# Turning the maxima of the half chunk with 128-row products, and inverting the column sums once

## The chip, the cores and the metric

The kernel runs on one core of a Trainium2 chip. A core has engines that run side by side and meet only at semaphores: TensorE (PE in the profile) multiplies matrices and writes to PSUM; VectorE (DVE) and ScalarE (ACT) compute elementwise and reduce, and carry results from PSUM to SBUF; GpSimd (POOL) computes on SBUF and issues most DMAs here; SyncE (SP) issues the rest. Each engine takes its instructions in the order in which the program lists them. The metric is the time of one execution on the device in microseconds (us).

## The reference

Attention with an extra term in the denominator, for 8 batches of 12 heads, 448 tokens and 64 dimensions, and then a mixture of experts with soft slots (8 experts of 4 slots, 768 wide, hidden layer of 1024), over the 3584 tokens of all batches.

```python
scores = scale * np.matmul(q, k.transpose(0, 1, 3, 2))
m = np.max(scores, axis=-1, keepdims=True)
e = np.exp(scores - m)
attn = e / (np.sum(e, axis=-1, keepdims=True) + np.exp(-m) + 1e-09)
x = np.matmul(attn, v)                       # then (batch, token) x (head, dim)

logits = x @ phi                             # 3584 x 32
d = np.exp(logits - logits.max(0, keepdims=True))
d /= d.sum(0, keepdims=True) + 1e-09
slot_input = (d.T @ x).reshape(E, S_per_e, D)
slot_out[e] = np.maximum(slot_input[e] @ w1[e], 0.0) @ w2[e]
c = np.exp(logits - logits.max(1, keepdims=True))
c /= c.sum(1, keepdims=True) + 1e-09
out = c @ slot_out
```

The maximum `m` of each row of scores and the sum of `c` over the 32 slots are what the change touches.

## The kernel before

**Tiles.** Heads are taken in pairs: 48 pairs `n`, six for each batch, and three pairs make a group `g` (`NP = 3`). The two heads of a pair (`hl` 0 and 1) lie in the two halves of the 128 partitions. The 448 rows of a head are cut into three chunks of 128 and one of 64; the 64-row "half chunks" of the two heads share one tile, head 0 in partitions 64 to 127 and head 1 in 0 to 63.

**Steps for a pair.** `T` turns q and k (TensorE L251, evicted by VectorE L257 or ScalarE L255). `A` and `A1` compute scores by row into `ps_a` (L274, L283, L291), from which VectorE takes the row maxima (`reduce_max`, L277, L285, L292) into one column of `wm`. `wm` has 4 x 128 columns for a group: chunk `i` in columns 128 `i` onward, head `hl` at 64 `hl`, pair `n % 3` behind that. Two `wm` tiles alternate; both are zeroed once at the start. `Bk` and `AB` compute the scores once more, turned, into `ps_b` (L337, L359), subtract the maxima by a product with `sel` (L340, L362), and ScalarE takes the exponential (L343, L364). `AV` multiplies by v (L397), `N1` evicts (L409), `N2` takes the reciprocal of the row sums on VectorE (L418, L419) and scales on POOL (L423, L427, L428), and `PX` turns the result (L449, evicted at L455).

**Turning the maxima.** Once for each group (17 times) `W2` turns `wm` into rows: three products with `ident` (L299) for the 128-row chunks, each a weight tile of 128 rows and 128 columns, and two products of 64 rows and 64 columns (L302) for the half chunk, one for each head. `W3` copies the result to `mT` (ScalarE L307) and computes the extra term of the denominator (`ec`, L311, L314).

**Work per batch.** `P(b)` holds the router's steps: logits (L475), their maxima, exponentials, sums for the slots (L543), and `c_turn`: TensorE turns the exponentials `cd` (L548), VectorE copies them to `cT` (L549), sums them over the slots into `crec[:, b, :]` (L551), adds 1e-9 (L552) and takes the reciprocal (L553). `crec` is 128 x 8 batches x 4 in fp32. It is read only after the hidden layer of the experts, by the products of L840 which move it to `cscale`.

**Order.** The whole order is written out by hand. A loop over `s` (48 pairs) with two half-steps `y` emits, in this order, `AB` and `Bk` for pair `s`, `A1` for a later pair between their products, `T(s + 6)`, and at `y = 1`, for every third `s`, `W2` and `W3` of the next group; then `AV` of pair `s`, then the step of `P` that `post` lists for this half-step, then `PX(s - 2)` and `N2`. `c_turn` of batches 0 to 5 falls in the half-step of `s = 6b + 11`, which has a `W2` as well. After the loop come the last batch's steps, the experts (`hidden`, `turn`, `slots`, `pick`) and the output. PSUM has 3 buffers for `ps_a` and `ps_t` (psA), 4 for `ps_b`, `ps_m` and `ps_x` (psB), and one for `ps_av`.

Of the kernel before, what the change touches and what calls it, by code (L numbers as in the profile page):

```python
# [10 lines left out]
AX = mybir.AxisListType  # L11
AF = mybir.ActivationFunctionType
ALU = mybir.AluOpType
# [12 lines left out]
NP = 3  # L26
W65 = 65
VS = 66


@with_exitstack
def kernel(
# [10 lines left out]
    nc = tc.nc  # L43
    B, H, S, D = q.shape
# [11 lines left out]
    scale = 1.0 / (D ** 0.5)  # L56
# [9 lines left out]
    crec = keep.tile([128, B, 4], F32, name="crec")  # L66
    acc = keep.tile([128, KC + 1, NS], F32, name="acc")

    ident = const.tile([128, 128], BF16, name="ident")
# [8 lines left out]

    NQK, NE, VPN, NATV = 7, 5, HG * 4 * VS, HG * 4 * D
    sizes = [("nq0", 2 * NP * S), ("nq1", 2 * NP * S), ("nv", NATV), ("qk6", 2 * S), ("wm1", 512),  # L80
# [13 lines left out]
    wm = [part(f"wm{i}", 0, 512).rearrange("p (i c) -> p i c", i=4) for i in range(2)]  # L94
# [48 lines left out]
    with ExitStack() as at:  # L143
# [118 lines left out]
        mg = lambda n: 0 if n == 0 else n // NP + 1  # L262

        def top(n, i, hl=0):
            c = 64 * hl + n % NP
            return wm[mg(n) % 2][:, i, c:c + 1]

        def A(n, i):
            t = qkT[n]
            if i < 3:  # L270
                pss = [psA.tile([128, 512], F32, tag="a", name="ps_a") for _ in range(2)]
                for hl in range(2):
                    r = slice(64 * hl, 64 * hl + 64)
                    nc.tensor.matmul(pss[hl][:, 0:S], t[r, 0, i * 128:(i + 1) * 128], t[r, 1, :],  # L274
                                     start=True, stop=True)
                for hl in range(2):
                    nc.vector.reduce_max(top(n, i, hl), pss[hl][:, 0:S], axis=AX.X)  # L277
            else:
                ps = psA.tile([128, 512], F32, tag="a", name="ps_a")

                for hl in range(2):
                    r = slice(64 * hl, 64 * hl + 64)
                    nc.tensor.matmul(ps[64 - 64 * hl:128 - 64 * hl, 0:S], t[r, 0, 384:448], t[r, 1, :],  # L283
                                     start=True, stop=True)
                nc.vector.reduce_max(top(n, i), ps[:, 0:S], axis=AX.X)  # L285

        def A1(n, i, hl):

            t, r = qkT[n], slice(64 * hl, 64 * hl + 64)
            ps = psA.tile([128, 512], F32, tag="a", name="ps_a")  # L290
            nc.tensor.matmul(ps[:, 0:S], t[r, 0, i * 128:(i + 1) * 128], t[r, 1, :], start=True, stop=True)  # L291
            nc.vector.reduce_max(top(n, i, hl), ps[:, 0:S], axis=AX.X)  # L292


        def W2(g):
            w = wm[g % 2]
            ps = pb_("ps_m")
            for i in range(3):
                nc.tensor.matmul(ps[:, i * 128:(i + 1) * 128], w[:, i, :], ident, start=True, stop=True)  # L299
            for hl in range(2):  # L300
                r = slice(64 - 64 * hl, 128 - 64 * hl)
                nc.tensor.matmul(ps[64 * hl:64 * hl + 64, 384:448], w[r, 3, 0:64], ident[r, r], start=True, stop=True)  # L302
            st["ps_m"] = ps

        def W3(g):
            t = psm.tile([128, S], BF16, tag="mT", name="mT")
            nc.scalar.copy(t, st["ps_m"][:, 0:S])  # L307
            mT[g] = t
            e = psm.tile([128, NP, 7], F32, tag="ec", name="ec", bufs=3)
            w = wm[g % 2]  # L310
            nc.scalar.activation(e[:, :, 0:6].rearrange("p l (i h) -> p i l h", i=3),  # L311
                                 w[:, 0:3, :].rearrange("p i (h c) -> p i c h", h=2)[:, :, 0:NP, :],
                                 AF.Exp, scale=-scale)
            nc.scalar.activation(e[:, :, 6], w[:, 3, 0:NP], AF.Exp, scale=-scale)  # L314
            ec[g] = e


# [144 lines left out]
        def P(b):  # L462
# [3 lines left out]
            v = {}  # L466
# [79 lines left out]
            def c_turn():  # L546
                ps = pa([128, 128], BF16, "ps_ct")
                nc.tensor.transpose(ps, flat(v["cd"][:, 0:4, :]), ident)  # L548
                nc.vector.tensor_copy(cT[:, b // 2, :, b % 2, :], ps.rearrange("p (h j) -> p h j", h=2))  # L549
                r = crec[:, b, :]  # L550
                nc.vector.reduce_sum(r, v["cd"][:, 0:4, :], axis=AX.X)  # L551
                nc.vector.tensor_scalar(r, r, 1e-9, None, op0=ALU.add)  # L552
                nc.vector.reciprocal(r, r)  # L553

            def s_add():
                if b:
# [68 lines left out]
        warm(1, S)  # L625
        As(2)
        W2(0)
        W3(0)
        V(0)
        load(1, "v")  # L630
# [15 lines left out]
        for s in range(NPAIR):  # L646
            for y in range(2):
# [18 lines left out]
                if y == 0:  # L666
                    if 0 <= s - 1:
                        for i in (2, 3):
                            AV(s - 1, i, range(3))
                else:  # L670
                    if 2 <= s < NPAIR - 6:
                        T(s + 6)
                    g = (s + 1) // 3
                    if (s + 1) % 3 == 0 and g < NG:
                        W2(g + 1)
                        W3(g + 1)
                    if s < NPAIR:
                        for i in (0, 1):
                            AV(s, i, range(3))
# [19 lines left out]
                if hs == 1:  # L699
                    W2(1)  # L700
                    W3(1)
# [26 lines left out]
        n = NPAIR - 1  # L728
# [107 lines left out]
        for half in range(2):  # L836
            ps = psA.tile([128, 512], F32, tag="a", name="ps_cs")
            r = slice(64 * half, 64 * half + 64)
            for b2 in range(2):
                nc.tensor.matmul(ps[64 * b2:64 * b2 + 64, 0:2 * B], identf[r, r], crec[r, b2::2, :],  # L840
                                 start=True, stop=True)
# [54 lines left out]
```

## Time and profile before

| | us |
|---|---|
| median of three runs | 308.73 |
| their range | 307.33 to 309.12 |
| the profiled execution | 309.52 |
| its span, first to last instruction | 307.7 |

| stage (us of the span) | length | TensorE busy | VectorE busy | ScalarE busy | POOL busy |
|---|---|---|---|---|---|
| first pairs (0 to 40) | 40 | 37.0 | 34.3 | 27.0 | 27.4 |
| 40 to 240 | 200 | 196.3 | 188.2 | 189.0 | 147.5 |
| 240 to 260 | 20 | 19.3 | 13.4 | 17.3 | 10.0 |
| experts (260 to 280) | 20 | 17.4 | 9.0 | 7.9 | 0.0 |
| output (280 to 308) | 28 | 9.3 | 12.2 | 9.9 | 0.0 |

The stages are sums of the profile's windows. From 40 to 240 us, where the pairs follow one another, three engines are busy for 94% of the time or more, and TensorE's granted clock is full. "Busy" for TensorE counts a product until it has left the array, so that products in flight together count once, and a wait shorter than that tail does not show as idle. VectorE and ScalarE overlap the tail of one instruction with the head of the next by 0.08 to 0.15 us when the second does not depend on the first.

### The profile page before, as it was taken

The numbers are of one execution on the slowest core, as the hardware profiler recorded it, in microseconds if no ns is written. First come the engines' busy times: TensorE is split into PE (matmuls) and PEld (weight loads), VectorE is DVE, ScalarE is ACT, GpSimd is POOL, SyncE is SP. The second block draws the span as 40 slices with busy tenths as digits, with TensorE's granted clock in tenths as the row PEclk, the third lists the DMA queues.
The fourth block names the chain that finished last, engine by engine and source line by source line (L and its number), as shares of the span: only waits on it lengthen the run. The fifth ranks groups of instructions, "written<-read, shape, count | busy, mean of one in ns | idle before, by whom it ended". The sixth has DMA issues, their size and how long they took to land.

```text
span 307.7 us, 12173 instructions
## 1 busy us (share of the span) xinstructions
PE 279.3 (91%) x5097; PEld 159.8 (52%) x5097; DVE 257.1 (84%) x604; ACT 250.9 (82%) x551; POOL 184.9 (60%) x336
## 2 busy tenths in 40 slices
PE   7999999999999999999999999999999999995900
PEld 2444656566565656555656565656564555441100
DVE  7899999999999999989999999999999676446910
ACT  3477999999999999989999999999999995345800
POOL 9681986968586869866877677686747662000000
PEclk9999999999999999999999999999999999997555
DMA  8999999999999999999999999999845899909995
GB/s 134 134 158 184 139 210 202 195 197 165 191 161 198 164 200 148 202 184 151 120 202 134 197 179 204 151 200 205 141 56 88 124 137 224 362 32 341 433 426 229
DMA packets 49384, 57.69 MB, mean 188 GB/s; under 512 B 2865, under 2 KB 41521, under 8 KB 48945
## 3 DMA queue, kind: packets, MB, share of 16 engines
q0 software_dynamic: 45280, 42.29, 89.6%
q1 hardware_dynamic: 4048, 14.62, 12.1%
q8 instruction: 40, 0.66, 0.8%
q14 instruction: 16, 0.12, 0.1%
HBM read 88.18 MB, written 14.16 MB: 333 GB/s over the span
## 4 chain that ended last, share of the span: by engine, by line
PE 69%; DVE 14%; ACT 8%; issue 3%; POOL 1%; DVEq 0%; POOLq 0%
PE ps_av L397 15%; PE ps_a L291 9%; PE ps_t L251 7%; PE ps_b L359 7%; PE ps_b L362 6%; DVE R L292 6%; PE ps_b L337 4%; PE ps_b L340 2%; ACT R L343 2%; DVE R L277 2%; PE ps_x L449 2%; PE ps_o L802 2%; PE ps_a L274 2%; PE ps_so L773 2%; ACT R L255 2%
## 5 line engine op out<-in xcount | busy, mean ns | idle before, releaser
L292 DVE TENSOR_REDUCE R<-ps_a 128x1 bf16<-128x448 f32 x254 | 140.0, 615 | 6.4 <-PE ps_a L291 5.5
L364 ACT ACTIVATE R<-ps_b 128x448 bf16<-128x448 f32 x272 | 131.0, 573 | 0.5 <-PE ps_b L362 0.2
L291 PE MATMUL ps_a<-R 64*128 64x448 bf16 x254 | 83.2, 353 | 1.5 <-DVE R L292 1.5
L359 PE MATMUL ps_b<-R 64*128 64x448 bf16 x272 | 74.5, 353 | 1.1
L362 PE MATMUL ps_b<-mT,sel 64*128 64x448 bf16 x272 | 71.3, 350 | 0.0
L423 POOL TENSOR_TENSOR R<-ubuf,rec 128x384 bf16<-128x384 f32 x44 | 36.2, 823 | 55.1 <-DVE rec L419 33.7
L397 PEld LDWEIGHTS <-R 128*128 128x128 bf16 (+1 forms) x1536 | 50.0, 100 | 30.8 <-issue 26.1
L397 PE MATMUL ps_av<-R 128*128 128x65 bf16 (+1 forms) x1536 | 64.6, 196 | 0.0
L343 ACT ACTIVATE R<-ps_b 128x448 bf16<-128x448 f32 x64 | 35.9, 579 | 2.7 <-PE ps_b L340 2.6
L251 PEld LDWEIGHTS <-R 64*64 64x64 bf16 x1344 | 30.0, 112 | 12.6 <-issue 4.9
L455 ACT CAST R<-ps_x 128x512 bf16<-128x512 f32 x47 | 28.1, 599 | 6.9 <-PE ps_x L449 6.4
L251 PE MATMUL ps_t<-ident,R 64*64 64x64 bf16 x1344 | 31.2, 196 | 0.6
L285 DVE TENSOR_REDUCE R<-ps_a 128x1 bf16<-128x448 f32 x48 | 29.6, 617 | 0.6 <-PE ps_a L283 0.6
L362 PEld LDWEIGHTS <-sel 64*128 64x128 bf16 x272 | 21.8, 94 | 15.1 <-issue 5.5
L291 PEld LDWEIGHTS <-R 64*128 64x128 bf16 x254 | 23.8, 94 | 11.1 <-issue 1.1
L409 ACT COPY ubuf<-ps_av 128x455 f32<-128x455 f32 x44 | 25.1, 570 | 2.4 <-POOL R L428 2.2
L255 ACT COPY R<-ps_t 128x896 bf16<-128x896 bf16 x20 | 18.4, 922 | 6.0 <-PE ps_t L251 5.6
L337 PE MATMUL ps_b<-R 64*64 64x448 bf16 (+1 forms) x112 | 21.9, 375 | 0.0
L277 DVE TENSOR_REDUCE R<-ps_a 128x1 bf16<-128x448 f32 x34 | 18.9, 618 | 2.1 <-PE ps_a L274 2.0
L340 PE MATMUL ps_b<-mT,sel 64*64 64x448 bf16 (+1 forms) x112 | 20.5, 353 | 0.0
L428 POOL TENSOR_TENSOR R<-ubuf,rec 128x128 bf16<-128x128 f32 x44 | 17.5, 398 | 3.7
L359 PEld LDWEIGHTS <-R 64*128 64x128 bf16 x272 | 17.2, 94 | 4.7 <-issue 0.3
(137 smaller groups left out, 439.7 us busy)
## 6 DMA issues: line engine op xcount, KB each, us to landing
W<-in_moe_w_dram POOLq DMA_DIRECT2D x22, 768.0 KB, 10.2
R<-in_v_dram POOLq DMA_DIRECT2D x32, 192.0 KB, 4.9
out_dram<-W SPq DMA_DIRECT2D x2, 2688.0 KB, 11.8
R<-in_q_dram POOLq DMA_DIRECT2D x14, 336.0 KB, 7.9
R<-in_k_dram POOLq DMA_DIRECT2D x14, 336.0 KB, 9.0
wd<-in_moe_w_dram POOLq DMA_DIRECT2D x8, 384.0 KB, 10.7
R<-wd SPq DMA_DIRECT2D x8, 384.0 KB, 8.2
R<-in_moe_w_dram POOLq DMA_DIRECT2D x2, 768.0 KB, 8.1
```

The source lines that it names most:

```text
L251: nc.tensor.transpose(ps[r, a, c:c + 64], src[r, pl, tok * D:(tok + 1) * D], ident[r, r])
L285: nc.vector.reduce_max(top(n, i), ps[:, 0:S], axis=AX.X)
L291: nc.tensor.matmul(ps[:, 0:S], t[r, 0, i * 128:(i + 1) * 128], t[r, 1, :], start=True, stop=True)
L292: nc.vector.reduce_max(top(n, i, hl), ps[:, 0:S], axis=AX.X)
L337: nc.tensor.matmul(outs[hl], t[rs[hl], 1, cols], t[rs[hl], 0, :], start=True, stop=False)
L343: nc.scalar.activation(e, p[:, 0:S], AF.Exp, scale=scale)
L359: nc.tensor.matmul(ps[hl][:, 0:S], t[rs[hl], 1, cols], t[rs[hl], 0, :], start=True, stop=False)
L362: nc.tensor.matmul(ps[hl][:, 0:S], sel[rs[hl], pl:pl + 1].to_broadcast([64, 128]), mT[mg(n)][rs[hl], :], start=False, stop=True)
L364: nc.scalar.activation(e[:, hl, :], ps[hl][:, 0:S], AF.Exp, scale=scale)
L397: nc.tensor.matmul(o, eT[n, i, hl][:, qc], vp[g % 2][:, 2 * pl + hl, i, 0:W65], start=(i == 0 and u == 0 and hl == 0), stop=(i == 3), skip ...
L423: eng.tensor_mul(x[:, 0:3, c:c + 128].rearrange("p i (h d) -> p i h d", h=2), u[:, 0:6, 0:D].rearrange("p (i h) d -> p i h d", h=2), rec[: ...
L455: nc.scalar.copy(xT[:, pb, :], pss[0])
```

## The change

Four edits in two places, and no instruction moves to another engine. In `top` the maxima of the half chunk go to columns 392 to 394 of `wm` instead of 384 to 386. In `W2` the two 64 x 64 products are replaced with two products over all 128 rows that add into the same 64 columns of PSUM. The first has columns 328 to 455 as weights (128 of them) and the first 64 columns of `ident` to stream, the second columns 392 to 511 (120 of them) and the other 64 columns of `ident`; both results are zero wherever `wm` was never written, so their sum puts head 1 at partitions 64 to 66 and head 0 at 0 to 2. `W3` reads the new columns. In `c_turn` the sums of each batch are kept as they are, and for the last batch alone the addition and the reciprocal run over all of `crec`, 32 columns.

```diff
+HALF = 392
...
         def top(n, i, hl=0):
-            c = 64 * hl + n % NP
-            return wm[mg(n) % 2][:, i, c:c + 1]
+            c = n % NP + (HALF if i == 3 else i * 128 + 64 * hl)
+            return wm[mg(n) % 2].rearrange("p i c -> p (i c)")[:, c:c + 1]
...
-            for hl in range(2):
-                r = slice(64 - 64 * hl, 128 - 64 * hl)
-                nc.tensor.matmul(ps[64 * hl:64 * hl + 64, 384:448], w[r, 3, 0:64], ident[r, r], start=True, stop=True)
+            f = w.rearrange("p i c -> p (i c)")
+            nc.tensor.matmul(ps[:, 384:448], f[:, HALF - 64:HALF + 64], ident[:, 0:64], start=True, stop=False)
+            nc.tensor.matmul(ps[0:512 - HALF, 384:448], f[:, HALF:512], ident[:, 64:128], start=False, stop=True)
...
-            nc.scalar.activation(e[:, :, 6], w[:, 3, 0:NP], AF.Exp, scale=-scale)
+            nc.scalar.activation(e[:, :, 6], w[:, 3, HALF - 384:HALF - 384 + NP], AF.Exp, scale=-scale)
...
-                r = crec[:, b, :]
-                nc.vector.reduce_sum(r, v["cd"][:, 0:4, :], axis=AX.X)
-                nc.vector.tensor_scalar(r, r, 1e-9, None, op0=ALU.add)
-                nc.vector.reciprocal(r, r)
+                nc.vector.reduce_sum(crec[:, b, :], v["cd"][:, 0:4, :], axis=AX.X)
+                if b == B - 1:
+                    nc.vector.tensor_scalar(crec, crec, 1e-9, None, op0=ALU.add)
+                    nc.vector.reciprocal(crec, crec)
```

The order of all instructions on each engine is otherwise the one of before.

## The prediction

> **What bounds the kernel now.** I read the page's busy times first, then its idle times by group, and then the chain of waits and the timelines around the two places that change.
>
> ```profile
> PE 279.3 (91%) x5097; PEld 159.8 (52%) x5097; DVE 257.1 (84%) x604; ACT 250.9 (82%) x551; POOL 184.9 (60%) x336
> ...
> L292 DVE TENSOR_REDUCE R<-ps_a 128x1 bf16<-128x448 f32 x254 | 140.0, 615 | 6.4 <-PE ps_a L291 5.5
> L364 ACT ACTIVATE R<-ps_b 128x448 bf16<-128x448 f32 x272 | 131.0, 573 | 0.5 <-PE ps_b L362 0.2
> ```
>
> No engine stands out. The largest VectorE group sits idle 6.4 us and the largest ScalarE group 0.5 us before its instructions. Three engines run nearly full side by side, so the shares don't say what an edit is worth. The chain of waits through the stretch in which both edits fall, 106.95 to 111.7 us, does:
>
> ```profile
> 107.27 0.27 PE ps_m L299 x3
> 107.54 0.15 PE ps_m L302 x2
> 107.69 0.47 PE ps_av L397 x12
> 108.16 0.07 PE ps_ct L548
> 108.23 0.02 issue
> 108.25 0.23 DVE cT L549
> 108.47 0.20 DVE crec L551
> 108.68 0.02 issue
> 108.70 0.18 DVE crec L552
> 108.88 0.02 issue
> 108.91 0.18 DVE crec L553
> 109.08 0.07 DVE rec L418
> 109.15 0.02 issue
> 109.17 0.20 DVE rec L419
> 109.37 0.50 DVE R L292
> 109.88 0.04 issue
> 109.92 0.35 PE ps_a L291
> ```
>
> The columns are start and length in us. The turned maxima (L299, L302) and the removed sums (L552, L553) all lie on the chain. TensorE's L291 at 109.92 waits for a psA buffer that VectorE's first L292 frees, and that L292 waits its turn behind crec.
>
> **Part 1, the turn of the maxima (W2).** The timeline of TensorE there:
>
> ```profile
> 107.20 0.34 PE L299 MATMUL ps_m<-ident,R 128*128 128x128 bf16 x3
> 107.47 0.22 PE L302 MATMUL ps_m<-ident,R 64*64 64x64 bf16 x2
> 107.62 0.54 PE L397 MATMUL ps_av<-R 128*128 128x65 bf16 x12
> ```
>
> The form after MATMUL is the tile of the array. Pitch (start to start): three L299 take 0.34 with 0.22 for one, so (0.34-0.22)/2 = 0.06. Twelve L397 take 0.54 with 0.19 for one, so (0.54-0.19)/11 = 0.03. The third L299 thus starts at 107.32. L302 starts 0.15 later instead of 0.06, and L397 0.15 after that: each change of the tile form, to 64\*64 and back, shows as a wait of about 0.15. From the first L299 to L397 it is 0.42 now.
>
> After the change all five products have the 128-row, 128-column form of their neighbours: 3 x 0.06, then two with 64 moving columns. For the first I take 0.03, the L397 row (65 moving columns, 128 of weights). The second has 120 columns of weights, which no row shows. Its bounds: 0.03, as L397; and 0.06, scaled from the transposes L251 (64 columns of weights, a pair in (0.63-0.19)/27 x 2 = 0.033, times 120/64). The form is nearest to L397 and only the count of columns differs, so I take 0.04. Sum: 0.18 + 0.03 + 0.04 = 0.25, so **0.17 less** per W2 (0.15 to 0.18).
>
> The Trainium skill, "TensorE: Matmul & The Clock Gate", sections "LDWEIGHTS (loading the stationary operand)" and "Weight-path perf modes — Fast Weight Load (FWL) and DoubleRow", speaks against this part: the fast load needs exactly 128 weights, and otherwise P columns cost P/1.2 ns, which would be 100 ns for 120. By that the second product takes 0.10, a W2 saves 0.11 and the whole change 4.0. The trace does not quite agree with the figure: it would make a 64-column load 53 ns, against 33 for a pair of L251.
>
> What follows each W2: the evictions wait for the last product, which starts at 0.21 after the first L299 instead of 0.27, so mT comes about 0.08 earlier. ScalarE's L307 has idle time ahead of it (L343 ends 107.58, L307 starts 107.73), and the next thing it waits for, ps_x (L455), moves the full 0.17. VectorE's L257 ends at 108.17 and overlaps its successor by 0.08, so VectorE can start the next piece at 108.09 instead of 108.25: up to 0.16 earlier, when both edits meet. Where W2 has no crec behind it (91.99 us), VectorE waits 0.17 for L500 plus the overlap, so it follows by the full 0.17.
>
> There are 17 W2 (51 L299). The first two (10.5 and 20.8 us) are followed by 64-row products, so one change of form stays, and from 15.71 VectorE runs L277 back to back: 0. The last, at 243.1, ends behind a busy ScalarE (L343 at 243.64, L307 only at 244.06): 0. Fourteen remain. Six share their half-step with crec. Of the other eight, the first two (33 and 47 us) have ScalarE nearly back to back around L307, so I take a little less for them, 0.15, and 0.17 for six: 6 x 0.17 + 2 x 0.15 = **1.3 us**.
>
> **Part 2, the column sums.** L552 and L553 go for seven of eight batches. Now L551 starts at 108.39, and L418, which doesn't need crec, starts at 109.00. Behind L551 (0.28, overlap 0.08 as L418 has behind L553) it starts at 108.59: **0.41 earlier**. That is more than 0.17 + 0.18, because the two dependent steps also have 0.03 idle each ahead of them and break the overlap. Then L419, the five L292, TensorE's L291 at 109.92 and, by way of POOL (L423 starts 0.16 after L419 ends, L428 follows), ScalarE's L409 all move.
>
> ```profile
> 111.14 0.54 ACT L409 COPY ubuf<-ps_av 128x455 f32<-128x455 f32 x1 [0.30 <-POOL R L428]
> ```
>
> This row sets how much of it ScalarE can take. L409 waits 0.30 for POOL and can overlap its predecessor by 0.13; with the 0.17 from W2 it can come at most 0.60 earlier. The sum asked is 0.16 + 0.41 = 0.57, so it fits, with 0.03 to spare. TensorE has room too: before L291 at 109.92 its sequence would run on at the 0.19 pitch (109.14 + 0.19 = 109.33), so 0.59 of wait is there now. It will arrive 0.17 earlier and be released 0.57 earlier, which leaves 0.19 of wait: VectorE still sets this place. POOL has been idle 3.06 us when L423 starts.
>
> The batches at 78.1, 108.4, 139.3, 169.6, 199.8 and 230.0 us (six L551 in that stretch) have this shape: 6 x 0.57 = **3.4 us**. The seventh, at 249.68, is followed by VectorE idle until 251: 0. In the eighth, at 266.07, the add and reciprocal grow from 4 to 32 columns. L549's 128 columns take 0.23, so each costs at most 0.06 more; VectorE waits 1.13 there before L765, so it is hidden. Without that cover it would be 0.1. What reads crec comes after 270.
>
> **Sum.** The profiled execution took 309.52, of which 307.7 are the span and 1.8 lie around it. Less 1.3 and 3.4: 309.52 - 4.7 = 304.8. The median of the runs shown is 308.73, 0.8 below that execution, so **304.0** for the new median. The bounds of the second wide product (0.15 or 0.18 per W2) move this by 0.2; losing the 0.03 of spare at L409 by another 0.2; the runs of before lie within 307.33 to 309.12, that is 0.9 either way. The forecast's own range is 302.8 to 305.2.
>
> **Rivals.**
> - *The tile form does not stay.* If 120 columns of weights count as another form, both waits of 0.15 come back around the second product: 0.18 to the first, then 0.15 and 0.15, that is 0.48 against 0.42, a loss of 0.06. Then eight W2 lose 0.06 and six batches gain 0.41 - 0.06: 2.1 - 0.5 = 1.6, so 307.1. For it: no row has 120. Against it: L299, L397 and L475 share the form with 128, 65 and 32 moving columns, so the moving side doesn't matter; only the weights' side is open.
> - *Only half of the sums' gain arrives,* because ScalarE takes over. It is at 0.5 us idle in its largest group, and in the crec half-steps it has 0.60 of room against 0.57. If it keeps to W2's 0.17 in these half-steps, all fourteen give about 0.16: 2.3, so 306.4. Against it is L409's row: its wait ends with POOL, whose work starts from L419.
> - *Hidden anyway:* 308.7, if the chain closes at something neither edit moves, as a load. For it: the DMA row reads 8 or 9 in nearly every slice to 230 us. Against: the largest wait for a load that is listed is 2.7 us in all, by POOL for v.
> - *Slower, by the clock.* TensorE is busy 1.66 and 1.45 of 2 us in 258 to 262 and has the full clock (1.00). If the new phase loses it there, the hidden layer and the slots (from the first L757 at 263.0 to about 275.2, 12.2 us at 1.00, TensorE busy 2.00 of 2 in most windows) run at 0.50, where the clock stands at the end now. All of it would cost 12.2: 308.7 - 4.7 + 12.2 = 316.2. It decides once more than 6.3 of these 12.2 us fall under the half clock (4.7 + 1.5 lost). Against it: the idle stretches before 262 keep their instructions, and the clock falls only at 280 to 282 (0.54), after a window with 0.82 of 2 us busy.
>
> **How the numbers follow.** Forecast 0.65; more than its own range, where the first and last W2 give something too, 0.05; tile form 0.08; half of the gain 0.10; hidden 0.07; slower 0.05. About 0.5% (1.5 us) is what a measurement of this kernel tells from no change, so faster means below 307.2. The tile-form case, at 307.1, lies on that line and is split evenly: faster 0.65 + 0.05 + 0.10 + 0.04 = 0.84; same 0.07 + 0.04 = 0.11; slower 0.05. The range reaches from 302.4 to 306.8: above the half-gain case, with the tile-form, hidden and slower cases (0.20) mostly left out.
>
> **What would show it.** In the timeline of TensorE: L299 to L397 in about 0.25 instead of 0.42, and no row in the 64\*64 form between. In VectorE's: L418 less than 0.25 after L551's start, against 0.61. In the chain through the crec half-step: the half-step shorter by nearly 0.6 us, L291 still waiting for L292 but by far less. Per batch (two W2, one crec) about 0.74 less. The prediction is wrong in part 1 if a gap of over 0.1 stands ahead of the second wide product, in part 2 if L409 on ScalarE no longer waits for POOL but for its own queue, and as a whole if the stretch after 240 us is longer than before.

## The result and the profile after

| | before | changed |
|---|---|---|
| median of 12 runs (us) | 309.33 | 305.04 |
| lowest to highest (us) | 307.33 to 311.32 | 303.09 to 307.30 |
| span of the profiled execution (us) | 307.7 | 303.1 |

The ratio of the times is 0.9863, with a 95% interval of 0.983 to 0.9896: 1.4% faster, 4.2 us of 309.33. Since a line was added near the top, a line of the old kernel has a number larger by one in the new (L299 is L300), with few exceptions in the edits themselves; in the experiments, the lines behind an edit move on by what it adds.

The page's first rows for the changed kernel, to set beside those of before:

```profile
PE 275.1 (91%) x5097; PEld 159.3 (53%) x5097; DVE 254.4 (84%) x590; ACT 249.3 (82%) x551; POOL 184.8 (61%) x336
...
L293 DVE TENSOR_REDUCE R<-ps_a 128x1 bf16<-128x448 f32 x254 | 139.9, 616 | 5.6 <-PE ps_a L292 5.1
L365 ACT ACTIVATE R<-ps_b 128x448 bf16<-128x448 f32 x272 | 131.2, 576 | 0.5 <-PE ps_b L363 0.2
```

The shares of busy time are as before: they told nothing of what the edits were worth, and they tell nothing now. The places do. TensorE's timeline at a W2, in the half-step of a `c_turn` (batch 1, before at 107.20):

```profile
105.95 0.34 PE L300 MATMUL ps_m<-ident,R 128*128 128x128 bf16 x3
106.12 0.19 PE L302 MATMUL ps_m<-ident,R 128*128 128x64 bf16 x1
106.15 0.22 PE L303 MATMUL ps_m<-ident,R 128*120 128x64 bf16 x1
106.21 0.53 PE L398 MATMUL ps_av<-R 128*128 128x65 bf16 x12
```

From the first L300 to the first L398 it takes 0.26 us; it was 0.42. No wait of 0.15 stands ahead of L302 or L303. The second wide product has a form of its own in the record, 128\*120, and lasts 0.22 instead of 0.19; L398 starts 0.06 behind it.

VectorE in the same half-step (before from 108.25):

```profile
106.84 0.22 DVE L550 COPY cT<-ps_ct 128x128 bf16<-128x128 bf16 x1
106.97 0.28 DVE L551 TENSOR_REDUCE crec<-cd 128x4 f32<-128x128 bf16 x1
107.16 0.16 DVE L419 SCALAR_TENSOR_TENSOR rec<-ubuf,ec 128x7 f32<-128x7 f32 x1
107.36 0.20 DVE L420 RECIPROCAL rec<-rec 128x7 f32<-128x7 f32 x1
107.47 3.23 DVE L293 TENSOR_REDUCE R<-ps_a 128x1 bf16<-128x448 f32 x6
```

L419 starts 0.19 behind the sum's start instead of 0.61. The chain of waits there, from 105.8 us on (start, length, what):

```profile
106.01 0.27 PE ps_m L300 x3
106.29 0.03 PE ps_m L302
106.32 0.06 PE ps_m L303
106.37 0.36 PE ps_av L398 x12
106.73 0.06 PE ps_ct L549
106.79 0.22 PE ps_x L450 x4
107.01 0.29 PE ps_a L292
```

VectorE is gone from the chain; TensorE follows TensorE to the end of the stretch. That must not be read as "VectorE is free", as TensorE's timeline behind it shows:

```profile
107.72 0.54 PE L363 MATMUL ps_b<-mT,sel 64*128 64x448 bf16 x2
108.10 0.35 PE L292 MATMUL ps_a<-R 64*128 64x448 bf16 x1
```

At the pitch of 0.19 the second L363 starts at 107.91, and L292 could start with it, as its neighbours do. It starts at 108.10, 0.05 after VectorE's first L293 has ended (at 108.05: 107.47 and 0.58), which frees its buffer. So 0.19 of wait for VectorE is left here, where 0.59 was before (by median of the six such places 0.20, and 0.59). The chain doesn't name it, since the wait is shorter than the 0.35 for which the product ahead of it still counts as busy.

**Pair-steps, by the trace.** The length from the first product of `Bk` of one pair (L337 before, L338 now) to the next pair's. This is one turn of the loop over `s`, two half-steps, and is called a pair-step here; the recorded expectations below call the same length a half-step. A column is one profiled execution, a row the median of its kind, in us, from 30 to 235 us:

| | before | changed | sums alone | turn alone |
|---|---|---|---|---|
| with W2 and crec (6) | 5.40 | 4.84 | 5.00 | 5.24 |
| with W2 alone (8) | 5.17 | 5.00 | 5.17 | 5.00 |
| without W2, the next after crec (6) | 4.63 | 4.63 | 4.64 | 4.63 |
| all others (21 or 22) | 5.06 | 5.06 | 5.06 | 5.06 |

(Of the eight, the first two are 4.82 and 4.87 long before, and also 0.17 shorter after.) Six lose 0.56 each, eight 0.17 each: 3.36 + 1.35 = 4.7 us. One pair-step, at 131 us before and 129 now, is 0.11 longer (below, under what was not expected). From the last L337 of all to the end it takes 52.5 us in both. That is the 4.6 us by which the span differs.

### The profile page after: what moved, and what is told of

It reads as the page before. It is cut to its first block, busy times and chain, and to the rows that moved or that the text cites. A ratio compares the mean times of both kernels' runs of the same rounds, so it can differ in the third digit from the quotient of the medians.

```text
span 303.1 us, 12159 instructions
## 1 busy us (share of the span) xinstructions
PE 275.1 (91%) x5097; PEld 159.3 (53%) x5097; DVE 254.4 (84%) x590; ACT 249.3 (82%) x551; POOL 184.8 (61%) x336
## 4 chain that ended last, share of the span: by engine, by line
PE 66%; DVE 15%; ACT 10%; issue 3%; POOL 0%; DVEq 0%; POOLq 0%
PE ps_av L398 14%; PE ps_a L292 9%; PE ps_b L360 7%; DVE R L293 6%; PE ps_b L363 6%; PE ps_t L252 6%; PE ps_b L338 4%; ACT R L344 3%; PE ps_x L450 2%; PE ps_b L341 2%; PE ps_o L803 2%; ACT R L256 2%; DVE R L278 2%; PE ps_so L774 2%; PE ps_h L758 2%
## 5 line engine op out<-in xcount | busy, mean ns | idle before, releaser
L293 DVE TENSOR_REDUCE R<-ps_a 128x1 bf16<-128x448 f32 x254 | 139.9, 616 | 5.6 <-PE ps_a L292 5.1
L365 ACT ACTIVATE R<-ps_b 128x448 bf16<-128x448 f32 x272 | 131.2, 576 | 0.5 <-PE ps_b L363 0.2
L292 PE MATMUL ps_a<-R 64*128 64x448 bf16 x254 | 82.8, 352 | 0.3 <-DVE R L278 0.2
L363 PE MATMUL ps_b<-mT,sel 64*128 64x448 bf16 x272 | 71.3, 350 | 0.1
L398 PEld LDWEIGHTS <-R 128*128 128x128 bf16 (+1 forms) x1536 | 50.6, 101 | 27.8 <-issue 23.7
L398 PE MATMUL ps_av<-R 128*128 128x65 bf16 (+1 forms) x1536 | 64.5, 196 | 0.0
L456 ACT CAST R<-ps_x 128x512 bf16<-128x512 f32 x47 | 28.1, 599 | 6.5 <-PE ps_x L450 6.5
L363 PEld LDWEIGHTS <-sel 64*128 64x128 bf16 x272 | 21.8, 94 | 15.3 <-issue 5.5
L292 PEld LDWEIGHTS <-R 64*128 64x128 bf16 x254 | 23.8, 94 | 11.0 <-issue 1.0
L410 ACT COPY ubuf<-ps_av 128x455 f32<-128x455 f32 x44 | 25.1, 571 | 0.6 <-POOL R L429 0.4
L256 ACT COPY R<-ps_t 128x896 bf16<-128x896 bf16 x20 | 18.5, 924 | 5.5 <-PE ps_t L252 5.1
L338 PE MATMUL ps_b<-R 64*64 64x448 bf16 (+1 forms) x112 | 22.0, 378 | 0.0
L429 POOL TENSOR_TENSOR R<-ubuf,rec 128x128 bf16<-128x128 f32 x44 | 17.5, 398 | 3.7
```

What stands on the lines that cost most here:

```text
L338: nc.tensor.matmul(outs[hl], t[rs[hl], 1, cols], t[rs[hl], 0, :], start=True, stop=False)
L363: nc.tensor.matmul(ps[hl][:, 0:S], sel[rs[hl], pl:pl + 1].to_broadcast([64, 128]), mT[mg(n)][rs[hl], :], start=False, stop=True)
L365: nc.scalar.activation(e[:, hl, :], ps[hl][:, 0:S], AF.Exp, scale=scale)
L398: nc.tensor.matmul(o, eT[n, i, hl][:, qc], vp[g % 2][:, 2 * pl + hl, i, 0:W65], start=(i == 0 and u == 0 and hl == 0), stop=(i == 3), skip ...
L456: nc.scalar.copy(xT[:, pb, :], pss[0])
```

## The experiments

All are compared with the kernel before on the same chip; the ratio is of times. Two undo one half of the change each.

**Turn alone.** The sums are inverted for each batch again:

```diff
-                nc.vector.reduce_sum(crec[:, b, :], v["cd"][:, 0:4, :], axis=AX.X)
-                if b == B - 1:
-                    nc.vector.tensor_scalar(crec, crec, 1e-9, None, op0=ALU.add)
-                    nc.vector.reciprocal(crec, crec)
+                r = crec[:, b, :]
+                nc.vector.reduce_sum(r, v["cd"][:, 0:4, :], axis=AX.X)
+                nc.vector.tensor_scalar(r, r, 1e-9, None, op0=ALU.add)
+                nc.vector.reciprocal(r, r)
```

> The 128-row turn of the maxima alone; the column sums are inverted for each batch as before. Theory (two changes of the tile form cost 0.16 us in each of 14 W2, and VectorE and ScalarE follow): half-steps with a W2 and no crec 5.17 -> 5.00 us, those with both 5.40 -> 5.24, in all about 2.3 us faster than before (ratio 0.9925). Rival (the sums carry the whole gain, and what TensorE gains in W2 it waits for VectorE later): half-steps as before, 0 to 0.5 us faster (ratio 0.999).

Measured: 0.9923 (0.9896 to 0.995); pair-steps 5.00 and 5.24, as the theory had it. In the crec pair-steps the chain of waits of this run goes by VectorE alone from 105.71 to 108.83; its start is:

```profile
106.24 0.53 DVE R L286
106.77 0.53 DVE R L258
107.30 0.13 DVE cT L550
107.43 0.20 DVE crec L552
```

L550 follows L258 at once; before, it started 0.07 after L257 had ended, as it waited for TensorE. So this is where W2's gain ends in these pair-steps, at 0.16: VectorE has no gap left there that a still earlier TensorE could close.

**Sums alone.** The half chunk is turned by the two 64 x 64 products again:

```diff
-            f = w.rearrange("p i c -> p (i c)")
-            nc.tensor.matmul(ps[:, 384:448], f[:, HALF - 64:HALF + 64], ident[:, 0:64], start=True, stop=False)
-            nc.tensor.matmul(ps[0:512 - HALF, 384:448], f[:, HALF:512], ident[:, 64:128], start=False, stop=True)
+            for hl in range(2):
+                r = slice(64 - 64 * hl, 128 - 64 * hl)
+                nc.tensor.matmul(ps[64 * hl:64 * hl + 64, 384:448], w[r, 3, HALF - 384:HALF - 320], ident[r, r], start=True, stop=True)
```

> The column sums inverted once alone; the half chunk is turned by two 64 x 64 products as before. Theory (the chain crec, rec, L292 sets the half-step of the six c_turn): L418's group starts 0.41 us earlier behind the sum, half-steps with crec 5.40 -> 4.99, all others as before, 2.5 us faster (ratio 0.992). Rival (ScalarE's L409 has only the 0.30 us for which it waits for POOL): half-steps 5.10, 1.8 us faster (ratio 0.994). Second rival (hidden): no change of the half-steps, ratio 1.0.

Measured: 0.992 (0.9881 to 0.9959); pair-steps 5.00 with crec (5.40 before), and 5.17 without, as before. The gain is 0.40, the theory's 0.41, and not the 0.30 for which L409 waited. ScalarE did follow: its row and the one ahead of it are

```profile
107.63 0.99 ACT L365 ACTIVATE R<-ps_b 128x448 bf16<-128x448 f32 x2
108.52 0.54 ACT L410 COPY ubuf<-ps_av 128x455 f32<-128x455 f32 x1
```

The pair of L365 ends at 108.62, 0.10 after L410 starts: the overlap makes up the rest. The two parts' gains, 0.40 and 0.16, add up to the 0.56 of both.

**Full weights.** `wm` has 520 columns (`wf` is all of them), so that the second wide product gets 128 columns of weights:

```diff
...
-            f = w.rearrange("p i c -> p (i c)")
+            f = wf[g % 2]
...
-            nc.tensor.matmul(ps[0:512 - HALF, 384:448], f[:, HALF:512], ident[:, 64:128], start=False, stop=True)
+            nc.tensor.matmul(ps[:, 384:448], f[:, HALF:HALF + 128], ident[:, 64:128], start=False, stop=True)
...
```

> The changed kernel with 520 instead of 512 columns in wm, so that the second wide product has 128 columns of weights instead of 120. Theory (the 120 columns are loaded more slowly, so that the product after it starts 0.055 us behind it instead of 0.03): it starts 0.03 behind, third L300 to first L398 0.115 instead of 0.14, 14 x 0.026 = 0.36 us faster than the changed kernel (ratio to before 0.985). Rival (the 0.055 belongs to the change from ps_m to ps_av or to adding into the same columns): stays 0.055, no difference.

Measured: 0.9847 (0.9817 to 0.9877). TensorE's timeline:

```profile
104.02 0.34 PE L301 MATMUL ps_m<-ident,R 128*128 128x128 bf16 x3
104.19 0.19 PE L303 MATMUL ps_m<-ident,R 128*128 128x64 bf16 x1
104.22 0.19 PE L304 MATMUL ps_m<-ident,R 128*128 128x64 bf16 x1
104.25 0.53 PE L399 MATMUL ps_av<-R 128*128 128x65 bf16 x12
```

L399 now follows 0.03 behind L304. The pair-steps with W2 alone fall from 5.00 to 4.97; those with crec stay at 4.84, although TensorE is 0.03 earlier there too. It waits longer for the buffer instead:

```profile
105.76 0.54 PE L364 MATMUL ps_b<-mT,sel 64*128 64x448 bf16 x2
106.17 0.35 PE L293 MATMUL ps_a<-R 64*128 64x448 bf16 x1
```

That is 0.22 (105.76 and 0.19, to 106.17), where the changed kernel waits 0.19; the six such places agree. So the 0.03 belonged to the 120 columns, and VectorE, not TensorE, sets the pair-step with crec. The time itself can't be told from that of the changed kernel.

**Narrow columns.** Two products over 128 rows with 64 columns of weights each:

```diff
-            nc.tensor.matmul(ps[:, 384:448], f[:, HALF - 64:HALF + 64], ident[:, 0:64], start=True, stop=False)
-            nc.tensor.matmul(ps[0:512 - HALF, 384:448], f[:, HALF:512], ident[:, 64:128], start=False, stop=True)
+            for hl in range(2):
+                nc.tensor.matmul(ps[64 * hl:64 * hl + 64, 384:448], f[:, HALF:HALF + 64],
+                                 ident[:, 64 - 64 * hl:128 - 64 * hl], start=True, stop=True)
```

> The changed kernel with the half chunk turned by two products of 128 rows and 64 columns of weights (one for each head), in place of the two wide ones. Theory (any change of the tile form costs about 0.15 us on the way in and out, whichever side is narrow): third L300 to first L398 about 0.27 to 0.30 us again, half-steps with a W2 and no crec 5.17 instead of 5.00, those with crec 5.00 instead of 4.84, as with the sums alone (ratio to before 0.992). Rival (only the 64-row side makes the wait): about 0.14, half-steps as in the changed kernel, ratio 0.986.

Measured: 0.9937 (0.9915 to 0.9959); pair-steps 5.17 and 5.01.

```profile
105.83 0.34 PE L300 MATMUL ps_m<-ident,R 128*128 128x128 bf16 x3
106.10 0.22 PE L303 MATMUL ps_m<-ident,R 128*64 128x64 bf16 x2
106.25 0.42 PE L399 MATMUL ps_av<-R 128*128 128x65 bf16 x8
```

From the first L300 to L399 it is 0.42 again, with waits of 0.15 on both sides. A form narrowed in its columns alone costs what one narrowed in rows and columns did. What the change removes is the change of form, not the half-used array.

**Late sum.** The sum itself (L551) is moved two half-steps of the loop on, into the next pair-step, for batches 0 to 5:

```diff
+                if b >= B - 2:
+                    c_sum()
+
+            def c_sum():
                 nc.vector.reduce_sum(crec[:, b, :], v["cd"][:, 0:4, :], axis=AX.X)
...
-                         both(exps, corr), both(s_mm, fade, s_add), c_turn]
+                         both(exps, corr), both(s_mm, fade, s_add), c_turn, c_sum]
...
```

> The changed kernel with the sum of c_turn (L551) moved two half-steps later for batches 0 to 5, to one in which ScalarE evicts the turned q and k and VectorE has 0.35 us idle. Theory (VectorE still sets the half-step of c_turn: TensorE waits 0.19 us for L293 there): these half-steps 4.84 -> 4.65, the later ones as before (4.63), 6 x 0.19 = 1.1 us faster than the changed kernel (ratio to before 0.983). Rival (the moved sum delays rec and with it POOL and ScalarE there): later half-steps 4.63 -> 4.82, no gain (0.986). Second rival (TensorE's own work sets the half-step of c_turn by now, as the chain of waits shows TensorE alone): 4.84 stays, no gain.

Measured: 0.9877 (0.983 to 0.9924), no gain. The pair-steps with crec fall to 4.77 instead of 4.65, and the next ones rise from 4.63 to 4.69. All three guesses were off in part. VectorE did set the 4.84, but only for 0.07 of it, as TensorE's and VectorE's timelines in the pair-step with crec show:

```profile
106.63 0.36 PE L292 MATMUL ps_a<-R 64*128 64x448 bf16 x1
107.40 0.53 PE L363 MATMUL ps_b<-mT,sel 64*128 64x448 bf16 x2
107.71 0.35 PE L292 MATMUL ps_a<-R 64*128 64x448 bf16 x1
```

```profile
106.85 0.20 DVE L420 RECIPROCAL rec<-rec 128x7 f32<-128x7 f32 x1
107.03 3.28 DVE L293 TENSOR_REDUCE R<-ps_a 128x1 bf16<-128x448 f32 x6
```

The wait at L292 shrinks from 0.19 only to 0.12 (107.40 and 0.19, to 107.71). VectorE's first L293 starts 0.18 behind the start of L420 instead of 0.12, in all six batches, because the product that it reads, the L292 of 106.63, ends only at 106.99: VectorE is no longer late there, and waits for TensorE itself. The chain from there into the next pair-step:

```profile
109.44 0.31 PE ps_b L338 x2
109.75 0.04 PE ps_a L284 x2
109.79 0.03 issue
109.82 0.18 ACT R L365
110.00 0.24 issue
110.24 0.61 ACT R L344
110.85 0.80 ACT R L256
111.65 0.50 ACT R L456
112.15 0.04 issue
112.19 0.35 PE ps_b L360
```

ScalarE enters the next pair-step with work left over, evicts the turned q and k (L256, 0.99 us in its own row), and TensorE waits for the ps_b buffer behind L456. In the changed kernel the same pieces of ScalarE lie on the chain there. The two pair-steps together take 9.47 in that kernel and 9.46 here: what the first gains, ScalarE takes back in the second.

**Split eviction, alone and with the late sum.** Both with 128 columns of weights; in every third pair the turned q and k go half by ScalarE, half by VectorE:

```diff
-            elif n < 8 or pl == 0:
+            elif n >= 8 and pl == 0:
+                nc.scalar.copy(t[:, 0, :], ps[:, 0, :])
+                nc.vector.tensor_copy(t[:, 1, :], ps[:, 1, :])
+            elif n < 8:
                 nc.scalar.copy(t, ps)
```

> The kernel with 128 columns of weights in both wide products, and in every third pair the turned q and k evicted half by ScalarE and half by VectorE instead of by ScalarE alone. Theory (in these half-steps without a W2 ScalarE sets the pace, TensorE waits 0.09 to 0.30 us for it there and VectorE has 0.34 idle): 13 half-steps of 4.50 to 4.70 lose these waits, 2.6 us faster in all at most (ratio to before 0.976 to 0.985). Rival (VectorE takes over, as it is the engine with the least room): no gain or up to 1 us slower than without (0.985 to 0.988).

> The split eviction and the late sum of c_turn together, with 128 columns of weights. Theory (ScalarE took what the late sum gave to VectorE; with ScalarE relieved the late sum pays): half-steps of c_turn 4.65 to 4.77 and the next ones no longer 0.07 longer, up to 0.6 us faster than the split alone. Rival (VectorE is full in the next half-step once it holds the copy and the sum): no faster than the split alone.

Measured: 0.9934 (0.991 to 0.9959) and 0.9951 (0.9923 to 0.9978), both slower than without the split (0.9847), and by more than the rival of the first had allowed. The pair-steps meant to gain went from 4.68 to 4.82 or 4.83. VectorE's row there, in the run without the late sum, shows a wait that was not there before:

```profile
98.92 0.39 DVE L258 COPY R<-ps_t 128x448 bf16<-128x448 bf16 x1 [0.22 <-ACT R L257]
```

The two halves (L257 and L258 here) don't run side by side: VectorE's copy starts after ScalarE's has ended, in all thirteen places, with 4.5 us of wait in all, and the VectorE queue behind it, rec and the maxima, is late. What makes the one copy wait for the other, no run tested. With the late sum, c_turn's pair-steps are 4.74, and those after them 5.04: it is no faster than the split alone, as the rival had it. No run beat the kernel with full weights, and that one lies within the interval of the changed kernel.

## Why the prediction was right

**The sum.** Forecast were 4.7 us less: 1.3 for W2 and 3.4 for the pair-steps with crec. The pair-steps of the trace gave 1.35 and 3.36. The span lost 4.6, the medians 4.3, the ratio says 4.2 (3.2 to 5.3). The predicted 304.0 lies 1.0 below the measured 305.04, and 0.6 of that is the starting point: 308.73 was the median of three runs, 309.33 that of twelve. The other 0.4, between 4.7 and the 4.3 of the medians, lies within the interval.

**W2.** 0.17 forecast, 0.16 measured from L300 to L398. The second wide product was taken at 0.04 between bounds of 0.03 and 0.06; the record gives 0.055 to the next product, near the upper bound. The Trainium skill, "TensorE: Matmul & The Clock Gate", section "Weight-path perf modes — Fast Weight Load (FWL) and DoubleRow", has the fast weight load on when the number of weights is 128; the trace agrees in kind, since the weight load of L303 takes 133 ns by median where those of L299 took 98, and the loss is gone with 128. The prediction's estimate from the Trainium skill's section "LDWEIGHTS (loading the stationary operand)", under the same title, was 100 ns for the step; it was 55. The pair-steps with W2 alone lost 0.17, a little more than the 0.16: after a change of form the first L397 also took 0.038 to the second, and 0.029 without. That the rounded 0.17 was met in full is partly luck, as the sum had not counted this.

**The tile form** (a rival) didn't come true: L303 is recorded as 128\*120, and yet no wait of 0.15 stands around it. The narrow columns, whose form does change, brought both waits back. The Trainium skill states in "TensorEngine Tiling (Array Packing)", section "Key Properties", that changing the tiling mode drains TensorE; the trace agrees, with a wait of 0.15 us each way.

**The sums.** 0.41 forecast behind the sum, 0.40 measured alone, and with W2's 0.16 the predicted 0.57 came as 0.56. The step that the two dependent instructions cost more than their 0.35 of busy time was right: without them L419 also overlaps the sum, by 0.09.

**The spare room of ScalarE** was put at 0.03. L410 now overlaps its predecessor by 0.09 (L365 ends at 109.42, L410 starts at 109.33), of 0.13 possible. The rival "only half of the sums' gain arrives" is excluded by the sums alone. The sign named for being wrong in part 2, that L409 no longer waits for POOL but for its own queue, seems to turn up, since the row of L410 has no idle time any more. POOL's row shows that it did not:

```profile
108.89 0.40 POOL L429 TENSOR_TENSOR R<-ubuf,rec 128x128 bf16<-128x128 f32 x1
```

L429 ends at 109.29, and L410 starts 0.04 behind it; before, L428 ended at 111.11 and L409 started 0.03 behind. So ScalarE still waits for POOL. With so little room left this wait lies under the tail of L365 and can't show as idle.

**TensorE's wait at L292** (L291 before) was to shrink from 0.59 to 0.19, and the timeline of the changed kernel has 0.19. That VectorE sets this place is also what full weights (0.03 of gain became wait) and the late sum (0.07 of gain, until VectorE waited for TensorE's product) show.

**One size was off, where it was hidden.** The last inversion was bounded at 0.06 more for each of the two instructions at 32 columns:

```profile
261.78 0.18 DVE L553 TENSOR_SCALAR crec<-crec 128x32 f32<-128x32 f32 x1
262.00 0.35 DVE L554 RECIPROCAL crec<-crec 128x32 f32<-128x32 f32 x1
263.29 0.69 DVE L766 COPY W<-ps_ht 128x1024 bf16<-128x1024 bf16 x1 [0.94 <-PE ps_ht L765]
```

The addition kept to it, the reciprocal grew from 0.18 to 0.35. The row used for the bound, a copy, was the wrong neighbour. It cost nothing, as VectorE still waits 0.94 for TensorE behind it.

**The clock and hidden rivals** didn't come true either: 52.5 us from the last L337 to the end in both profiles, so nothing was lost or gained there. (The 6.3 us named in the clock's case is 6.2 by its own terms, 4.7 + 1.5.) The granted clock falls in the output stage in both. In the changed kernel's profile it also reads half in the second of the 40 slices (7.6 to 15 us). That seems to cost up to 2 us: the loop's first pair-step with a W2 begins at 32.4 us there, but at 30.4 in the profile of full weights and at 30.6 in that of the sums alone, in which the clock reads full in this slice. In the profile before it begins at 32.4 us as well. The clock reads full there, yet the 28 transposes L251 at 11.88 us take 0.89 on the chain of waits, against 0.56 at 19.57 us. So both profiles are late by as much, which is luck, and only therefore do their spans differ by what the pair-steps gave. What the first two W2 gave, which were put at nothing, can't be told from this; the last gave nothing, as forecast: its pair-step takes 4.41 before and 4.40 now.

## What to carry to other kernels

Where three engines are all busy, follow the chain through the very stretch of an edit and ask of each engine how far it can move before its own queue holds it; the smallest of these rooms is the gain, and here it was right to 0.02 us in each pair-step. A small product in another tile form cost little by itself here and 0.15 us on either side of it; padding it with zeros to its neighbours' form was cheaper. A chain of tiny dependent instructions on a nearly full engine cost more than its busy time (0.40 for 0.35), and it can be batched to the end when its reader is far away. A wait that is shorter than the tail of the instruction ahead shows in no list of idle times; look at starts and ends instead.

## What the runs showed that was not expected

**A reciprocal goes by its columns.** 178 ns for 4 columns, 353 for 32: 6.3 ns for each further column between these two sizes, while the addition on the same operands hardly grew (0.17 to 0.18 us).

**Stalls that the profile doesn't explain.** At 133 us of the profile before, TensorE stands still in the middle of the products of L543, and at 131 us in the changed kernel:

```profile
130.53 0.60 PE L544 MATMUL ps_s<-cd,R 128*128 128x32 bf16 x18
131.88 0.32 PE L544 MATMUL ps_s<-cd,R 128*128 128x32 bf16 x6 [0.74 <-issue]
```

"issue" means that the engine waited for nothing that the profile shows. Counted in recorded products from the start, it is the same place, number 2398, in the profiles before, of the change, of the turn alone, of full weights and of narrow columns, and 0.66 to 0.94 us from one product's start to the next; the late sum has 0.49 there, the sums alone and the two runs with the split none as long. Others are at 2270 in full weights, 1502 in the late sum (there the profile names VectorE's L293, though no other batch of that run has such a wait), 3166 and 3422 in the narrow columns, 990 and 1374 in the split with the late sum: all whole multiples of 128 products from 2398. Since each product has a weight load of its own, 128 products are 256 instructions. That may point to blocks of the instruction stream that arrive late, but no run took this apart. Together with the start (the first pair-step with a W2 began between 30.4 and 32.4 us in the profiles without the split) the stalls are part of why single spans differ by more than the pair-steps do.
